# Two-part stores of the mirrored features in a fused attention, Fourier and MLP kernel

## Chip, cores and metric

One core of one Trainium2 chip runs the whole program in one launch. The metric is the device time of an execution in microseconds (us). Everything is float32 in DRAM; matmul operands are float32, or pairs of reduced-precision parts ("hi" and "lo", called h and l in the names).

## What is computed

```python
def _attn_ref(q, k, v, tau):                      # 4 batches, 8 heads, 576 rows, 64 columns
    scores = scale * np.matmul(q, k.transpose(0, 1, 3, 2))
    thresh = np.max(scores, axis=-1, keepdims=True) - tau
    scores = np.where(scores >= thresh, scores, -1000000000.0)
    ...
    return np.matmul(attn, v).astype(np.float32)

def _moe_ref(x, w_ch1, w_ch2):                    # x: 4 x 576 x 512
    X = np.fft.fft(x, axis=1)
    X = np.fft.fft(X, axis=2)
    u = x + np.real(X).astype(np.float32)
    ...
    un = (u - mu) / np.sqrt(var + 1e-06)
    ch = np.maximum(un @ w_ch1, 0.0) @ w_ch2      # 512 -> 2048 -> 512
    return (u + ch).astype(np.float32)

def _moe2_ref(x, w_val, conv_w, w_out):
    ...
    return (gate * val @ w_out).astype(np.float32)  # gate: sigmoid of a 5-tap convolution
```

## The kernel before

Features lie on partitions, sequence positions on the free axis. Attention runs first, in 16 head pairs (`p`, four to a batch `b`) of 9 score tiles each. A tile (`g_tile`) is scores on TensorE (`s`, L686), row maximum on VectorE (`neg`, L751), exponential on ScalarE (`e`, L757), threshold and sum on VectorE (`p`, L768), scaling on GpSimd (`p`, L776), transposes on TensorE (`t`, L788) and a copy to SBUF (`m`, L805). `g_pv` then multiplies with the values (L455), and ScalarE copies the result into `xt` (L460), 128 features by 576 positions.

When the four pairs of a batch are there, `g_fold` and `g_fft` make the real part of the two-dimensional Fourier transform. Symmetry halves it: features 0 to 255 and the features that mirror them, 256 to 511 in the kernel's own order, come out of the same two products (L598): their difference `dd` and sum `sm` (L628, L630). `g_odd` reads a block of 128 attention features back from DRAM (`xd`, L654) and its mirrored block (`xr`, L655), adds `dd` and `sm` on GpSimd (L634 and L636 into `xd`, L639 and L641 into `xr`) and stores both to `u_d[b]`, a DRAM buffer of 512 features by 576 positions (L637 and L643). There are two blocks to a batch, `j` = 0 and 1. Row 0 of the mirrored block 0 is feature 256, the middle one, which belongs to another path (`g_ny`, L616); so for `j` = 0 the store L643 leaves row 0 out and carries 127 rows, 2,304 bytes each.

In batches 0 to 2 the tiles of `j` = 1 use the same buffers as those of `j` = 0: the loads L654 and L655 of `j` = 1 must wait until the stores L637 and L643 of `j` = 0 have landed. In batch 3 `j` = 1 has buffers of its own.

The MLP's weights come from DRAM in 32 pieces by GpSimd's queue (`raw`, L945), are split into hi and lo on VectorE, ScalarE and GpSimd (L280 to L290), and those of the first 16 pieces are stored (`e_h`, `e_l`, L969) and loaded again into the weight tiles `w0h`, `w0l`, `w1h`, `w1l` (L929) as soon as attention's buffers come free. Chunk 0 of the MLP (512 positions) is woven into the end of attention and of batch 3's Fourier transform: `h` (L1258) needs `w0h` and `w0l`, `c` (L1294) needs `w1h` and `w1l`. Four more chunks (L1104, L1120), the gate and the output product (L1492, L1510) follow, TensorE running through.

The order of instructions on each engine is set when the program is built: a planner (`Loom`) with costs and due times writes it once, and no cost of it depends on the DMAs of L643. All DMAs but those of GpSimd are issued by SyncE (SP), which takes its list strictly in order: an entry that waits holds all that stand behind it. SP's DMAs rotate through eight completion semaphores, so that each also waits until the one eight before it has landed.

Of the kernel before, what the change touches and what calls it, by code (L numbers as in the profile page):

```python
# [23 lines left out]
DM = H * D  # L24
# [50 lines left out]
def dve(n, fast=False):  # L75
    return 137.0 + (0.54 if fast else 1.055) * n
# [242 lines left out]
def attention_fft(tc, right, ps_f, a, u_d, dram, conv_w, loom):  # L319
    nc = tc.nc  # L320
    PE, DVE, ACT, POOL, SP = nc.tensor, nc.vector, nc.scalar, nc.gpsimd, nc.sync
    right1 = ExitStack()
    with ExitStack() as right2, ExitStack() as right2b, ExitStack() as right3, ExitStack() as right4, ExitStack() as scores, ExitStack() as turned:
# [208 lines left out]
        def g_fft(b):  # L532
# [68 lines left out]
            def buffers(j):  # L601
                if b < B - 1 or j == 0:
                    return ([fft_p.tile([128, S], F32, tag=nm, name=nm) for nm in ("xd", "xr")]
                            + [fft_p.tile([128, KE], F32, tag=nm, name=nm) for nm in ("ws", "dd", "sm")])
                wide = [f32(fft_p.tile([128, 2, KE], F32R, tag=nm, name=nm)) for nm in ("xeh", "xel", "xoh", "xol")]
                return [t.rearrange("p a b -> p (a b)")[:, 0:S] for t in wide[:2]] + [wide[2][:, 0], wide[2][:, 1], wide[3][:, 0]]
# [18 lines left out]
            def g_odd(j, f, room, x, xr, ws, dd, sm):  # L625
                yield "after", ("ws", b, j)
                yield "DVE", dve(KE), 0.25
                DVE.tensor_tensor(out=dd, in0=ws, in1=f[:, 0:KE], op=ALU.subtract)  # L628
                yield "DVE", dve(KE), 0.25
                DVE.tensor_tensor(out=sm, in0=ws, in1=f[:, 0:KE], op=ALU.add)  # L630
                loom.free(room)
                up, dn, md = slice(0, HALF + 1), slice(S - 1, HALF, -1), slice(1, HALF)
                yield "POOL", 860.0, 3, "port"
                POOL.tensor_tensor(out=x[:, up], in0=x[:, up], in1=dd[:, up], op=ALU.add)  # L634
                yield "POOL", 780.0, 3, "port"
                POOL.tensor_tensor(out=x[:, dn], in0=x[:, dn], in1=sm[:, md], op=ALU.add)  # L636
                SP.dma_start(out=u_d[b][j * 128:(j + 1) * 128], in_=x)  # L637
                yield "POOL", 860.0, 3, "port"
                POOL.tensor_tensor(out=xr[:, up], in0=xr[:, up], in1=sm[:, up], op=ALU.add)  # L639
                yield "POOL", 780.0, 3, "port"  # L640
                POOL.tensor_tensor(out=xr[:, dn], in0=xr[:, dn], in1=dd[:, md], op=ALU.add)  # L641
                r = int(j == 0)
                SP.dma_start(out=u_d[b][DM // 2 + 128 * j + r:DM // 2 + 128 * j + 128], in_=xr[r:])  # L643
                loom.mark("added", b, j)

            yield ("after", *[("part", b, k, nb) for k in range(2) for nb in range(3)])
# [3 lines left out]
            for j in range(2):  # L650
                if j and b < B - 1:
                    yield "after", ("added", b, 0)
                x, xr, ws, dd, sm = buffers(j)
                SP.dma_start(out=x, in_=xs[j * 128:(j + 1) * 128])  # L654
                SP.dma_start(out=xr, in_=rev[j * 128:(j + 1) * 128])  # L655
                if b % 2 and j == 0:
                    ny = fft_p.tile([2, S], F32, tag="ny", name="ny")
                    for i, t in enumerate((ny_d, rev)):
                        SP.dma_start(out=ny[i:i + 1], in_=t[0:1])
                    f, room = yield from stage2(False, slice(0, CE, CE - 1))  # L660
                    loom.add(g_ny(f, room, ny))
                f, room = yield from stage2(False, slice(1 + j * 128, 129 + j * 128))
                loom.add(g_even(j, f, room, ws))
                f, room = yield from stage2(True, slice(j * 128, j * 128 + 128))
                loom.add(g_odd(j, f, room, x, xr, ws, dd, sm))
# [1017 lines left out]
```

## Time and profile before

| | us |
|---|---|
| median of 3 runs | 859.88 |
| lowest, highest run | 858.81, 861.76 |
| profiled execution, its time | 858.65 |
| its span, first to last instruction | 856.9 |
| TensorE busy (share of the span) | 817.6 (95%) |
| VectorE, ScalarE, GpSimd busy | 561.7, 418.0, 380.1 |
| mean granted clock of TensorE | 0.993 |

The profile is of one execution, with an entry for every instruction. A wait of an engine is the time that it stood still before an instruction, with the event that ended it; "<-" reads "by". In a timeline a row is a start, a length, the engine, the line, what is written from what, and how many were merged into the row. SP's rows show when it issued a DMA, not when the DMA landed; the landing shows where something waits for it.

### The profile page before, as it was taken

Reading aid. Unit: us, or ns where it says so; the run is one execution under the profiler, and the core shown is the slowest. Engines: PE = TensorE matmul, PEld = TensorE weight load, DVE = VectorE, ACT = ScalarE, POOL = GpSimd, SP = SyncE. Lnnn points to the kernel's source line nnn. Section 1 sums busy time; section 2 is a strip of 40 time slices with the busy share of each in tenths; the row PEclk is TensorE's granted clock in tenths of the full one; section 3 lists DMA queues with packets and bytes.
Section 4 is the critical chain, followed back from the end, with each engine's and each line's share of the span. In section 5 each row is a group of like instructions: output and inputs, shape, how many; then the busy total and the mean of one; then the engine's idle time right before and its main releaser. Section 6 shows DMA issues by size and latency. Waiting matters only on the chain.

```text
span 856.9 us, 13836 instructions
## 1 busy us (share of the span) xinstructions
PE 817.6 (95%) x4878; PEld 651.3 (76%) x4878; DVE 561.7 (66%) x1220; ACT 418.0 (49%) x845; POOL 380.1 (44%) x448
## 2 busy tenths in 40 slices
PE   8999999999889997999999999999999999999997
PEld 6555566556556754788899999998888788889986
DVE  7999899999898996688847732142123656328730
ACT  5778777777577774644545323133122331133432
POOL 4556864884688556475452431013003110075421
PEclk9999999999999998999999999999999999999999
DMA  6365365535534539968634622003000230532111
GB/s 214 106 211 186 104 184 176 185 131 194 188 111 154 211 95 362 370 228 294 219 129 168 218 60 66 1 24 113 1 1 10 95 105 0 195 128 83 62 50 62
DMA packets 63661, 117.67 MB, mean 137 GB/s; under 512 B 14304, under 2 KB 21472, under 8 KB 63592
## 3 DMA queue, kind: packets, MB, share of 16 engines
q1 hardware_dynamic: 56248, 92.93, 32.3%
q0 software_dynamic: 7200, 23.86, 8.2%
q8 instruction: 39, 0.64, 0.3%
q14 instruction: 30, 0.25, 0.1%
q10 hardware_dynamic: 144, 0.00, 0.0%
HBM read 85.29 MB, written 31.47 MB: 136 GB/s over the span
## 4 chain that ended last, share of the span: by engine, by line
PE 70%; DVE 15%; ACT 5%; issue 5%; POOL 3%; DMA 2%; SPq 0%; DVEq 0%; ACTq 0%; POOLq 0%
PE c L1120 16%; PE h L1104 16%; DVE neg L751 6%; PE s L686 5%; PE f L455 5%; PE o L1510 5%; PE h L1258 5%; PE v L1492 5%; PE c L1294 4%; DVE p L768 4%; PE t L788 3%; ACT e L757 2%; PE f L598 2%; PE f L583 1%; DMA w0h<-e_h 1%
## 5 line engine op out<-in xcount | busy, mean ns | idle before, releaser
L776 POOL TENSOR_SCALAR p<-p,su 128x576 f32<-128x576 f32 x144 | 110.0, 773 | 87.8 <-DVE su L703 79.1
L1108 DVE SCALAR_TENSOR_TENSOR hl<-h,hh 128x384 fp32r<-128x384 f32 (+1 forms) x64 | 39.8, 622 | 147.4 <-ACT hh L1107 147.4
L1107 ACT ACTIVATE hh<-h 128x384 fp32r<-128x384 f32 (+1 forms) x64 | 34.9, 545 | 203.2 <-PE h L1104 202.9
L757 ACT ACTIVATE e<-s,neg 128x576 f32<-128x576 f32 x144 | 102.2, 742 | 53.9 <-DVE neg L751 47.9
L768 DVE SCALAR_TENSOR_TENSOR p<-s,thr,e 128x576 f32<-128x576 f32 x144 | 112.2, 815 | 8.4 <-POOL p L776 0.2
L751 DVE TENSOR_REDUCE neg<-s 128x1 f32<-128x576 f32 x144 | 102.7, 748 | 8.7 <-PE s L686 8.0
L686 PE MATMUL s<-kt,qt 64*128 64x288 f32 (+1 forms) x640 | 97.8, 440 | 9.3 <-DVE p L768 8.7
L1120 PE MATMUL c<-hl,w1h 128*128 128x384 f32 (+1 forms) x256 | 92.9, 363 | 0.2 <-DVE hl L1108 0.2
L1120 PE MATMUL c<-hh,w1h 128*128 128x384 f32 (+1 forms) x256 | 92.6, 362 | 0.0
L1120 PE MATMUL c<-hh,w1l 128*128 128x384 f32 (+1 forms) x256 | 92.6, 362 | 0.0
L788 PE MATMUL t<-ident,p 128*128 128x128 f32 x464 | 69.3, 282 | 13.8 <-ACT m L805 9.8
L686 PEld LDWEIGHTS s<-kt,qt 64*128 64x128 f32 (+1 forms) x640 | 45.9, 175 | 47.0 <-issue 17.7
L788 PEld LDWEIGHTS t<-ident,p 128*128 128x128 f32 x464 | 50.9, 142 | 36.3 <-issue 17.4
L455 PE MATMUL f<-m,v 128*64 128x320 f32 (+1 forms) x512 | 68.8, 410 | 0.2 <-ACT th L723 0.2
L805 ACT ACTIVATE m<-t 128x512 f32<-128x512 f32 x116 | 66.0, 599 | 1.1 <-PE t L788 0.6
L1104 PE MATMUL h<-unh,w0h 128*128 128x384 f32 (+1 forms) x256 | 61.6, 362 | 0.0
L1104 PE MATMUL h<-unh,w0l 128*128 128x384 f32 (+1 forms) x256 | 61.6, 362 | 0.0
L1104 PE MATMUL h<-unl,w0h 128*128 128x384 f32 (+1 forms) x256 | 61.5, 362 | 0.0
L1129 POOL TENSOR_TENSOR res<-ht,res 128x512 f32<-128x512 f32 (+1 forms) x20 | 23.0, 1187 | 84.5 <-DVE ht L1128 84.5
L455 PEld LDWEIGHTS f<-m,v 128*64 128x64 f32 x512 | 34.0, 137 | 25.8 <-issue 3.6
L1120 PEld LDWEIGHTS c<-hl,w1h 128*128 128x128 f32 x256 | 48.1, 188 | 6.1 <-DVE hl L1108 1.2
L1120 PEld LDWEIGHTS c<-hh,w1l 128*128 128x128 f32 x256 | 48.0, 188 | 5.0
(268 smaller groups left out, 1701.2 us busy)
## 6 DMA issues: line engine op xcount, KB each, us to landing
raw<-in_moe_w_ch POOLq DMA_DIRECT2D x32, 512.0 KB, 6.6
qt<-in_q SPq DMA_DIRECT2D x15, 576.0 KB
kt<-in_k SPq DMA_DIRECT2D x15, 432.0 KB
ypad<-y_d SPq DMA_DIRECT2D x16, 288.0 KB
out<-os SPq DMA_DIRECT2D x18, 256.0 KB
v<-in_v SPq DMA_DIRECT2D x16, 256.0 KB
e_h<-cx SPq DMA_DIRECT2D x16, 256.0 KB
e_l<-ct SPq DMA_DIRECT2D x16, 256.0 KB
```

Source lines behind the costliest of these rows:

```text
L455: PE.matmul(out=f[h * 64:h * 64 + 64, 0:n], lhsT=w, rhs=r, start=(t == 0), stop=(t == 4))
L686: PE.matmul(out=s[o, c, 0:HALF], lhsT=qt[w, hh, q], rhs=kt[w, 2 if h == 2 and hh else hh], start=True, stop=True)
L751: DVE.tensor_reduce(out=neg[u][:, j, 0:1], in_=sc[g][:, :, 0:HALF], axis=AX.XY, op=ALU.max, negate=True)
L757: ACT.activation(e, sc[g][:, :, 0:HALF], AF.Exp, bias=neg[u][:, j, 0:1], scale=1.0)
L768: DVE.scalar_tensor_tensor(out=p_view(g).rearrange("p (a b) -> p a b", a=2), in0=sc.pop(g)[:, :, 0:HALF], scalar=thr[u][:, j:j + 1], in1=e ...
L776: POOL.tensor_scalar(out=v, in0=v, scalar1=ssum[u][:, j:j + 1], scalar2=1.0, op0=ALU.mult, op1=ALU.mult)
L788: PE.matmul(out=f[:, t, :], lhsT=pv[:, t * 128:(t + 1) * 128], rhs=ident, is_transpose=True, start=(t == 0), stop=(t == 3))
L805: ACT.activation(o, fv, AF.Copy)
L1104: PE.matmul(out=f[:, 0:n], lhsT=ww[:, k * 128:(k + 1) * 128], rhs=x[:, k, 0:n], start=(i == 0), stop=(i == 3 * KB - 1))
L1120: PE.matmul(out=ch[c][o][:, 0:n], lhsT=ww[:, o * 128:(o + 1) * 128], rhs=x, start=(at_ == 0 and i == 0), stop=(at_ == FB - 1 and i == 2))
L1258: PE.matmul(out=f[:, 0:n], lhsT=ww[:, k * 128:(k + 1) * 128], rhs=x[:, k, 0:n], start=(i == 0), stop=(i == 3 * KB - 1))
L1492: PE.matmul(out=f[:, 0:HALF], lhsT=w[:, k, o * 128:(o + 1) * 128], rhs=x[:, k, s], start=(i == 0), stop=(i == 3 * KB - 1))
```

## The change

The one store of rows 1 to 127 becomes two, rows 1 to 15 and rows 16 to 127. The same bytes go to the same place; for `j` = 1 the slice is the whole tile, as before.

```diff
-                r = int(j == 0)
-                SP.dma_start(out=u_d[b][DM // 2 + 128 * j + r:DM // 2 + 128 * j + 128], in_=xr[r:])
+                for r in ([slice(1, 16), slice(16, 128)] if j == 0 else [slice(0, 128)]):
+                    SP.dma_start(out=u_d[b][DM // 2 + 128 * j:][r], in_=xr[r])
                 loom.mark("added", b, j)
```

In the built program the instructions of TensorE, VectorE, ScalarE and GpSimd stand in the same order as before. SP's list gets one entry more in each of the four batches.

SP's list in batch 2, before, from the store of `j` = 0 on. (`DMAHW` are the eight completion semaphores; `PE`, `Pool`, `DVE`, `Activation` are counters of the engines. The number at a name tells buffers apart.)

```order
L643 DMA u_d_59<-xr 127x576 [waits DMAHW3_49,Pool_49]
L654 DMA xd<-xs_2634 128x576 [waits DMAHW6_49,DMAHW4_49]
L655 DMA xr<-xr_2635 128x576 [waits DMAHW7_49,DMAHW5_49]
L390 DMA v_195<-in_v 128x512 [waits DMAHW0_49,PE_49]
L392 DMA vt_196<-in_vt 64x64 [waits DMAHW1_49,PE_49]
L392 DMA vt_196<-in_vt 64x64 [waits PE_49]
L487 DMA xr_3651<-xt 128x576 [waits Activation_49]
```

L655 holds SP here until the store above it has landed (DMAHW5), and everything below it with it.

The same place in the changed program:

```order
L643 DMA u_d_59<-xr 15x576 [waits DMAHW5_49,Pool_49]
L643 DMA u_d_59<-xr 112x576 [waits DMAHW0_49]
L654 DMA xd<-xs_2635 128x576 [waits DMAHW6_49,DMAHW1_49]
L655 DMA xr<-xr_2636 128x576 [waits DMAHW7_49,DMAHW2_49,DMAHW0_49]
L390 DMA v_195<-in_v 128x512 [waits DMAHW3_49,PE_49]
```

L655 now waits for the landing of both parts (DMAHW2 and DMAHW0); nothing else has moved.

What follows on SP, from the changed program (in the program before, the same entries in the same order; only the semaphores are counted on by one):

```order
L969 DMA e_h<-cx 128x512 [waits DVE_49]
L969 DMA e_l<-ct 128x512 [waits Pool_49]
L474 DMA mirror<-xr_3653 128x576 [waits DMAHW6_49,DMAHW1_49]
L474 DMA mirror<-xr_3653 128x576 [waits DMAHW2_49]
L929 DMA w0h_4216<-e_h 128x512 [waits DMAHW3_49]
L929 DMA w1l_4219<-e_l 128x512 [waits PE_49]
L637 DMA u_d_59<-xd 128x576 [waits DMAHW7_49,Pool_49]
L643 DMA u_d_59<-xr 128x576 [waits DMAHW0_49,Pool_49]
L969 DMA e_h<-cx 128x512 [waits DMAHW1_49,DVE_49]
L969 DMA e_l<-ct 128x512 [waits DMAHW2_49,Pool_49]
L495 DMA xs_3652<-xt 128x576 [waits DMAHW3_49,Activation_49]
L929 DMA w0h_4337<-e_h 128x512 [waits DMAHW4_49]
```

The engine counters in it name these instructions: the first `e_l` waits for GpSimd's L290 of the same piece, `w1l` for the last scores of attention (L686), the stores L637 and L643 of `j` = 1 for L636 and L641, the second `e_l` for the next L290, `xs` for ScalarE's copy L460 of pair 14. The last row, `w0h` of the second weight group, is the load that the second `h` (L1258) needs.

## Rows read from the trace of the kernel before

**Rows 1.** The page's busy times by engine.

```profile
PE 817.6 (95%) x4878; PEld 651.3 (76%) x4878; DVE 561.7 (66%) x1220; ACT 418.0 (49%) x845; POOL 380.1 (44%) x448
```

**Rows 2.** TensorE's waits from 326 to 860 us: total, times, longest.

```profile
PE h L1258 <- DMA w0h<-e_h: 5.0, 1, 5.0
PE f L583 <- ACT sp L560: 1.0, 1, 1.0
```

**Rows 3.** The chain that ended last, 300 to 345 us: start, us, what.

```profile
329.75 9.32 DMA w0h<-e_h
...
339.12 4.92 PE h L1258 x12
```

**Rows 4.** Busy time by engine in stretches, then granted clock, DMA share, GB/s.

```profile
139.40:153.30 13.90, 13.09 (x100) 8.94 (x101) 12.56 (x33) 11.27 (x25) 7.42 (x10) 1.00 0.19 65
...
329.70:334.00 4.30, 4.30 (x24) 2.71 (x20) 4.30 (x6) 3.67 (x8) 3.21 (x5) 1.00 1.04 406
334.00:339.10 5.10, 0.13 (x1) 0.00 (x0) 3.47 (x4) 1.21 (x3) 4.40 (x7) 0.74 1.04 399
```

**Rows 5.** The same for L1258 alone (TensorE, weight loads, clock, DMA).

```profile
339.10:343.90 4.80, 4.79 (x12) 3.60 (x12) 0.57 1.05 395
...
376.10:378.90 2.80, 2.77 (x12) 2.10 (x12) 1.00 0.96 358
```

**Rows 6.** SP's waits over the whole span: total, times, longest.

```profile
SPq L655 <- DMA u_d<-xr: 26.6, 3, 9.1
...
SPq L474 <- DMA xr<-xt: 6.0, 2, 5.3
```

**Rows 7.** SP's timeline in batch 2 (start, length of the issue, line, DMA).

```profile
301.91 0.32 SPq L637 DMA_DIRECT2D u_d<-xd  x1
303.31 0.24 SPq L643 DMA_DIRECT2D u_d<-xr  x1
303.99 4.35 SPq L654 DMA_DIRECT2D xd<-xs  x1
317.14 0.32 SPq L655 DMA_DIRECT2D xr<-xr  x1
...
329.14 0.46 SPq L495 DMA_DIRECT2D xs<-xt  x1
329.75 0.58 SPq L929 DMA_DIRECT2D w0h<-e_h  x1
```

**Rows 8.** GpSimd's waits, 139 to 170 us.

```profile
POOL kt L381 <- DMA kt<-in_k: 1.2, 1, 1.2
```

**Rows 9.** GpSimd's timeline, 300 to 400 us.

```profile
313.36 1.04 POOL L290 TENSOR_TENSOR ct<-raw 128x512 fp32r<-128x512 f32 x1
...
318.00 0.80 POOL L634 TENSOR_TENSOR xd<-xd,dd 128x289 f32<-128x289 f32 x1 [0.49 <-DMA xd<-xs]
...
321.02 0.96 POOL L639 TENSOR_TENSOR xr<-xr,sm 128x289 f32<-128x289 f32 x1 [1.58 <-DMA xr<-xr]
...
324.67 1.20 POOL L290 TENSOR_TENSOR ct<-raw 128x512 fp32r<-128x512 f32 x1
```

**Rows 10.** TensorE's timeline, 300 to 341 us.

```profile
315.74 1.40 PE L686 MATMUL s<-kt,qt 64*128 64x288 f32 x12
...
323.87 0.66 PE L788 MATMUL t<-ident,p 128*128 128x128 f32 x4 [0.43 <-POOL p L776]
324.75 0.66 PE L788 MATMUL t<-ident,p 128*128 128x128 f32 x4 [0.23 <-POOL p L776]
...
333.06 1.07 PE L1258 MATMUL h<-unl,w0h 128*128 128x512 f32 x4
```

**Rows 11.** ScalarE's timeline, 316 to 380 us.

```profile
323.48 0.44 ACT L460 ACTIVATE xt<-f 128x320 f32<-128x320 f32 x1 [1.59 <-PE f L455]
...
344.07 0.60 ACT L1270 ACTIVATE hh<-h 128x512 fp32r<-128x512 f32 x1 [8.62 <-PE h L1258]
```

**Rows 12.** VectorE's timeline, 316 to 380 us.

```profile
344.70 0.69 DVE L1272 SCALAR_TENSOR_TENSOR hl<-h,hh 128x512 fp32r<-128x512 f32 x1 [6.76 <-ACT hh L1270]
```

## Prediction

> **What bounds the kernel now.** I read the page's busy times first: TensorE is busy 817.6 us of the 856.9 of the span [rows 1], so a change that touches no engine's work can pay only where TensorE stands still, or where its clock is low. TensorE's waits from the end of attention on are next [rows 2]: one of 5.0 us, before the second `h` (L1258), ended by the DMA that brings `w0h`; the next longest is 1.0 us, in the 520 us behind it. The chain that ended last runs through the same place: the load of `w0h` stands in it with 9.32 us, and the `h` behind it with 4.92 us for 12 matmuls [rows 3]. The stretch table tells the rest of that pause. While TensorE rests, DMA is full (share 1.04, 399 GB/s) [rows 4]; after it the 12 matmuls take 4.79 us at a granted clock of 0.57, close to the 1.2 GHz level, where the same 12 take 2.77 us at 1.00, the 2.4 GHz level, later [rows 5]. So the pause costs 5.0 us and then 4.79 - 2.77 = 2.0 us of low clock: 7.0 us.
>
> Why does `w0h` come late? It was issued at 329.75 [rows 7], and SP issues in order. SP's own waits show that L655 waited three times for `u_d<-xr`, the 127-row store, 26.6 us together [rows 6]. In batch 2 the store was issued at 303.31 and L655 at 317.14, 13.8 us later; L654, between them, needed 4.35 us to issue [rows 7]. The 128-row store of the same bytes per row just before it, `u_d<-xd` at 301.91, had landed when L654, which waits for it, was issued at 303.99: at most 2.1 us [rows 7]. One row less takes over six times as long.
>
> **The change part by part.**
>
> *The store itself, batches 0 to 2.* Two DMAs instead of one. What a 15-row and a 112-row store take no row shows. From below: the 128-row store, 2.1 us [rows 7]. From above: 13.8 us, that of the 127 rows [rows 7]. I take 2 to 6 us: 128-row stores with other traffic beside them reach the 5.3 us that `mirror` waited for one [rows 6], and 112 rows are nearer to 128 than to 127 only if the number of DMA engines that share the rows decides; that is the one assumption of this forecast, and the rival below prices its failure. The Trainium skill gives a rule for just this (DMA: Bandwidth & Descriptors, the section "Why a DMA increments its semaphore by 16 and not by 1"): a DMA from SP is spread over the largest number of engines, up to 16, that divides its rows, so 127 rows go through one engine, 15 rows through 15 and 112 through 16. By that rule the value is the lower end; the 13.8 against 2.1 us agree with it, though no row here shows 15 or 112 rows.
>
> The extra issue costs SP 0.24 to 0.32 us [rows 7], hidden in the wait that it shortens. L655 in batch 2 then issues between 303.6 + 2.1 = 306 and 310, not at 317.14.
>
> *What holds SP next.* Behind L655, four things stand that do not depend on the store. The first `e_l` waits for GpSimd's L290, which ends at 313.36 + 1.04 = 314.4 [rows 9]; so whether L655 goes at 306 or 310 makes no difference. `w1l` waits for attention's last scores, 315.74 + 1.40 = 317.1 [rows 10]. The stores of `j` = 1 wait for L636 and L641: L634 began at 318.00 after 0.49 us for `xd`, L639 at 321.02 after 1.58 us for `xr` [rows 9], both loads that now land early, so that the L641 store comes at about 320.5. The second `e_l` waits for the next L290, which ended at 324.67 + 1.20 = 325.9 [rows 9] and comes some 2 us sooner with those waits gone; and `xs` waits for ScalarE's copy, 323.48 + 0.44 = 323.9 [rows 11], where it was issued at 329.14 [rows 7]. So `w0h` is issued at about 324.6 and not at 329.75: 5.1 us sooner. The 11 us at L655 are worth 5 at `w0h`.
>
> *When `w0h` lands.* It took 9.32 us with DMA full [rows 3, 4]. Had it the same now, it would land at 333.9; with an idle queue, by the 2.1 us above, at 326.7. What queued ahead of it (`mirror` twice, the first weight group, the stores, some 3 MB by their shapes) leaves from 314.4 on and no longer in a bunch after 317, so I take about 329. TensorE wants it at the end of the first `h`, 333.06 + 1.07 = 334.1 [rows 10], less what it gains before (next).
>
> *GpSimd's earlier scaling.* With 0.49 and 1.58 us less waiting [rows 9] GpSimd reaches L776 about 2 us sooner, and TensorE's two waits for it, 0.43 and 0.23 us [rows 10], go: -0.7 us. The first `h` then ends at 333.4.
>
> *Batches 0 and 1, and batch 3.* The same stall is covered there: TensorE is busy 13.09 us of the 13.90 between store and release in batch 0, VectorE 12.56 [rows 4], and of GpSimd's waits behind it only one names a load, `kt`, 1.2 us [rows 8]. I take 0, with 0 to 2 us for both. In batch 3 no load waits for the store, and TensorE does not wait behind it [rows 2]: 0. If that cover were gone, SP would still be sooner than before.
>
> *What is late next.* With the pause gone TensorE reaches everything behind it 7.7 us sooner. The engines that feed it there were waiting for it: ScalarE 8.62 us for `h` [rows 11], VectorE 6.76 us for ScalarE [rows 12]. They move with it. The next weights have to come sooner too: the DMAs whose issue the L655 wait pushed behind 317 are, by their shapes, seven blocks of 0.26 to 0.29 MB and the first weight group, 1.05 MB: some 3 MB, or 7.5 us at the 399 GB/s of the full queue [rows 4]. So DMA can follow by about as much as TensorE gains, with nothing much to spare. I charge 0, and up to 2 us for the range.
>
> **The sum**, against the profiled execution: 5.0 + 2.0 + 0.7 = 7.7 us less, 858.65 - 7.7 = 851.0. That execution lies 1.2 us under the median of the runs, 859.88; on the median's scale the forecast is 859.88 - 7.7 = **852.2 us**.
>
> **Rivals.**
>
> *A part of the pause stays.* `w0h` lands 9.32 us after its issue again, at 333.9 [rows 3], 0.5 us after TensorE wants it, or later weights come late, up to 2 us. For it speaks the full DMA [rows 4], against it the 5 us of unhurried queue before. If the clock falls in the short pause as it did in the long one, 7.7 - 0.5 - 2.0 = 5.2 us remain: about 854.7.
>
> *DMA takes it back.* From 329.7 the queue is full at about 400 GB/s [rows 4]. If the release moves up not 3 MB but 1 MB, because GpSimd and TensorE hold SP at the places named, TensorE gains 2.5 us at the next weights whatever happens at `w0h`: about 857.4. Against it: of the holds only two, 314.4 and 317.1, lie before the first weights, and both are sooner than the issues that they replace.
>
> *The change does not do what it says, and costs.* If the landing goes by rows and not by how they divide, 13.8 us for 127 is 0.11 us a row: 1.6 us for 15 rows and 12.2 for 112, one behind the other, and each with an end of its own, up to the 2.1 us of a whole short store [rows 7]. L655 then goes at 317.4 to 319.5, `w0h` follows by 0.3 to 2.3 us, and TensorE's pause grows from 5.0 to as much as 7.3: 860.2 to 862.2, slower; it decides as soon as L655 goes later than 317.14. Batches 0 and 1 are covered as now. Against it stands the 128-row store in 2.1 us. By the rule of the page named above it cannot be.
>
> *More than forecast.* The first two stalls give the 1.2 us of `kt` [rows 8] and as much again in batch 1: 849.8.
>
> **How the numbers follow.** About 0.3% (2.6 us) is what a measurement of this kernel can tell from no change. Chances: the forecast 0.67, part of the pause 0.13, more than forecast 0.08, DMA takes it back 0.07, slower store 0.05. The first three are faster by over 0.3%: 0.88. DMA's rival lies on the edge, 0.05 of it within and 0.02 over; the slow store is 0.03 within and 0.02 slower. So 0.90, 0.08, 0.02. The range for 8 in 10 goes from the last rival, 849.8, to the half pause with the scatter of the runs, 1.2 us, on it: 854.7 + 1.2 = 855.9.
>
> **What would show it.** Right: SP's wait of L655 for `u_d<-xr` falls from 26.6 us to under 10; L655 in batch 2 issues before 311; `w0h` of the second group issues near 324.6; TensorE's 5.0 us wait at L1258 is gone, and the 12 matmuls there take 2.8 us at a clock of 1.00. If L655 still waits some 9 us each time, the store is not faster and the first step fell. If `w0h` is early and TensorE pauses at a later `h` or `c`, DMA took it back. If all that holds and the time falls by less than 5 us, something behind 365 us lost it, which no row here shows.

## The result, and the profile after

The changed kernel takes 850.75 us (median of 4 runs, 850.53 to 851.17) against 859.43 us (4 runs of the kernel before beside it, 858.81 to 861.76): a ratio of 0.9895, 95% interval 0.9875 to 0.9914, or 7.4 to 10.7 us less. Between the medians it is 8.7 us; 7.7 us less were forecast. The profiled execution took 851.17 us, with a span of 849.4.

The page's busy times by engine: hardly an engine works less than before [rows 1]; the span is shorter.

```profile
PE 816.8 (96%) x4878; PEld 651.4 (77%) x4878; DVE 561.2 (66%) x1220; ACT 418.0 (49%) x845; POOL 381.2 (45%) x448
```

TensorE's waits from 318 to 855 us (what waits, for what: total, times, longest). The 5.0 us for `w0h` of [rows 2] are not there; the 1.0 us at L583 is now the longest:

```profile
PE f L583 <- ACT sp L560: 1.0, 1, 1.0
```

SP's waits over the span. L655's for the store fell from 26.6 us [rows 6] to 7.3. The wait for GpSimd's `ct`, 47.7 us before, took most of that over: SP is released earlier and then stands at the next thing that is not ready.

```profile
SPq L969 <- POOL ct L290: 62.5, 19, 10.4
...
SPq L655 <- DMA u_d<-xr: 7.3, 4, 2.7
```

SP's timeline in batch 2 (start, length of the issue, line, DMA), to be read against [rows 7]. All of it lies 1.2 us later in this execution than in the profile of before: the first store here begins at 303.12, there at 301.91.

```profile
303.12 0.32 SPq L637 DMA_DIRECT2D u_d<-xd  x1
304.53 0.76 SPq L643 DMA_DIRECT2D u_d<-xr  x2
305.38 0.39 SPq L654 DMA_DIRECT2D xd<-xs  x1
308.75 0.34 SPq L655 DMA_DIRECT2D xr<-xr  x1
...
315.63 0.32 SPq L969 DMA_DIRECT2D e_l<-ct  x1
...
318.42 0.44 SPq L929 DMA_DIRECT2D w1l<-e_l  x1
...
321.57 0.32 SPq L643 DMA_DIRECT2D u_d<-xr  x1
...
325.98 0.32 SPq L969 DMA_DIRECT2D e_l<-ct  x1
...
326.82 0.44 SPq L929 DMA_DIRECT2D w0h<-e_h  x1
...
333.45 0.32 SPq L969 DMA_DIRECT2D e_h<-cx  x1
```

L655 goes 4.2 us behind the store instead of 13.8, and L654 issues in 0.39 us instead of 4.35. The `w0h` of the second group follows at 326.82; on the clock of the profile of before, that is 325.6 instead of 329.75.

TensorE's timeline at the place of the pause (start, length, line, operation, count): the second `h` begins at 334.22, straight behind the first, and its 12 matmuls end at 336.94, 2.7 us later, where they took 4.79 us [rows 5].

```profile
333.30 1.08 PE L1258 MATMUL h<-unl,w0h 128*128 128x512 f32 x4
334.22 1.07 PE L1258 MATMUL h<-unh,w0h 128*128 128x512 f32 x4
...
336.94 0.39 PE L1294 MATMUL c<-hh,w1h 128*128 128x512 f32 x1
...
339.66 1.07 PE L1258 MATMUL h<-unh,w0h 128*128 128x512 f32 x4
```

The stretch table (length, busy times of PE, PEld, DVE, ACT, POOL, then granted clock, DMA share, GB/s), against [rows 4]: the DMAs run at 305 GB/s from 317.1 to 329.7 (275 in the profile of before), and when the queue is full from 334 on, TensorE is busy all the time at a clock of 1.00.

```profile
317.10:329.70 12.60, 12.39 (x108) 7.42 (x110) 12.01 (x23) 7.16 (x18) 9.63 (x12) 1.00 0.94 305
...
334.00:339.10 5.10, 5.10 (x24) 4.24 (x23) 4.45 (x7) 2.06 (x4) 4.40 (x6) 1.00 1.05 366
```

### The profile page after: what moved, and what is told of

Its sections match the earlier page's. It is cut to its first block, busy times and chain, and to the rows that moved or that the text cites. A ratio compares the mean times of both kernels' runs of the same rounds, so it can differ in the third digit from the quotient of the medians.

```text
span 849.4 us, 13837 instructions
## 1 busy us (share of the span) xinstructions
PE 816.8 (96%) x4878; PEld 651.4 (77%) x4878; DVE 561.2 (66%) x1220; ACT 418.0 (49%) x845; POOL 381.2 (45%) x448
## 4 chain that ended last, share of the span: by engine, by line
PE 70%; DVE 16%; ACT 4%; DMA 3%; POOL 3%; issue 3%; SPq 0%; DVEq 0%; ACTq 0%; POOLq 0%
PE c L1120 18%; PE h L1104 18%; DVE neg L751 6%; PE o L1510 5%; PE s L686 5%; DVE p L768 5%; PE v L1492 4%; PE c L1294 4%; PE f L455 4%; PE h L1258 4%; PE t L788 3%; ACT e L757 2%; PE f L598 1%; PE f L583 1%; DMA w0l<-e_l 1%
## 5 line engine op out<-in xcount | busy, mean ns | idle before, releaser
L686 PE MATMUL s<-kt,qt 64*128 64x288 f32 (+1 forms) x640 | 98.4, 441 | 8.9 <-DVE p L768 8.2
L686 PEld LDWEIGHTS s<-kt,qt 64*128 64x128 f32 (+1 forms) x640 | 46.1, 176 | 47.0 <-issue 17.1
```

The source lines that it names most:

```text
L686: PE.matmul(out=s[o, c, 0:HALF], lhsT=qt[w, hh, q], rhs=kt[w, 2 if h == 2 and hh else hh], start=True, stop=True)
```

## The experiments

Each edit is to the kernel before. The kernel before took 860.28 us (19 runs, 858.65 to 862.29) beside the runs of the first two groups, and 860.29 us (19 runs, 858.77 to 861.88) beside the 128-row store, the buffer of its own and the 20 extra matmuls.

### Two parts in batch 2 alone, and in the others alone

```diff
-                r = int(j == 0)
...
+                for r in ([slice(0, 128)] if j else [slice(1, 16), slice(16, 128)] if b == 2 else [slice(1, 128)]):
+                    SP.dma_start(out=u_d[b][DM // 2 + 128 * j:][r], in_=xr[r])
```

> Only batch 2 stores in two parts; batches 0, 1 and 3 keep the 127-row store. Theory (the gain comes through the weight load that batch 2's stall delays): all of it, about 851 us, TensorE's 5.0 us wait at L1258 gone, SP's two waits of L655 in batches 0 and 1 still about 9 us each. Rival (every one of the four stores gives its share): a quarter to a half of the gain, 855 to 857 us.

The other has `b != 2` there:

> Batches 0, 1 and 3 store in two parts; batch 2 keeps the 127-row store. Theory: no gain, 858.5 to 859.5 us, the 5.0 us wait at L1258 still there; the stalls of batches 0 and 1 vanish and nothing on TensorE moves by more than some tenths of a us. Rival (each store its share): 852 to 855 us.

Batch 2 alone: 852.2 us (4 runs), ratio 0.9915, 0.9891 to 0.9939. The others alone: 859.52 us (10 runs), ratio 0.9992, 0.9982 to 1.0002. So batch 2 carries the gain, and the others give between nothing and 1.5 us; 0.6 us of that lie, in the profile, at the very end of the program (see the account of the prediction). SP's timeline of the others alone in batch 2, and TensorE's wait:

```profile
304.80 0.24 SPq L643 DMA_DIRECT2D u_d<-xr  x1
...
318.68 0.32 SPq L655 DMA_DIRECT2D xr<-xr  x1
```

```profile
PE h L1258 <- DMA w0h<-e_h: 5.4, 1, 5.4
```

There SP's waits at L655 fell by half as well (26.6 to 13.9 us), and TensorE's pause stayed: what is saved at a wait counts only where somebody stands behind it.

### Two parts that divide badly: 14 + 113 rows, 5 + 122 rows

```diff
+                for r in ([slice(1, 15), slice(15, 128)] if j == 0 else [slice(0, 128)]):
+                    SP.dma_start(out=u_d[b][DM // 2 + 128 * j:][r], in_=xr[r])
```

> The stores in two parts as in the change, but cut one row further up: rows 1 to 14 and 15 to 127, 14 and 113 rows. Theory (the number of engines that a store runs on is the largest number up to 16 that divides its rows): 113 rows run on one engine, 113 x 0.109 = 12.3 us, so that L655 in batch 2 still goes some 12 us after the store and w0h comes 1 to 2 us sooner than before: 857 to 858.5 us, with a pause of 3 to 4 us at L1258. Rival (two smaller stores side by side, or not starting a long store at row 1, is what helps): as the change, about 851 us.

With `slice(1, 6), slice(6, 128)`:

> Rows 1 to 5 and 6 to 127, 5 and 122 rows. Theory: 122 = 2 x 61, two engines, 61 x 0.109 = 6.6 us, so that L655 in batch 2 goes some 7 us after the store, at about 311, still ahead of the hold of SP by GpSimd's L290 at 314.4: the full gain, about 851 us. Rival (the time goes with the length of the stall): half the gain, about 855 us.

14 + 113: 858.38 us (10 runs), ratio 0.9977, 0.9962 to 0.9992. 5 + 122: 852.44 us (4 runs), ratio 0.9905, 0.9890 to 0.9920. SP's timeline of 14 + 113, then of 5 + 122:

```profile
303.79 0.62 SPq L643 DMA_DIRECT2D u_d<-xr  x2
...
316.62 0.34 SPq L655 DMA_DIRECT2D xr<-xr  x1
```

```profile
303.91 0.58 SPq L643 DMA_DIRECT2D u_d<-xr  x2
304.63 0.34 SPq L654 DMA_DIRECT2D xd<-xs  x1
312.03 0.34 SPq L655 DMA_DIRECT2D xr<-xr  x1
...
315.17 0.48 SPq L969 DMA_DIRECT2D e_l<-ct  x1
...
326.22 0.44 SPq L929 DMA_DIRECT2D w0h<-e_h  x1
```

One row moved from the first part to the second brings the stall back: 12.8 us from store to L655, and a wait of 4.6 us at the second `h`, more than the 3 to 4 us expected. So it is not the cutting that helps. With 5 + 122 the stall is only cut to 8.1 us, yet the whole gain is there: L655 at 312.03 is just early enough, since SP reaches the `e_l` behind it at 315.17, 0.2 us after the L290 that it has to wait for in any case (313.96 + 1.03). `w0h` issues 22.3 us behind the store, as with 15 + 112 (326.82 - 304.53).

Times alone leave a rival open: the larger part starts at row 1, 15, 6, 16 or 0 where it has 127, 113, 122, 112 or 128 rows, and as the two add up to 128, the start divides by 2, 4, 8 or 16 just where the count does. The trace settles it. SP's queue (packets, MB, share of 16 engines) from 311 to 312.5 us of before, with the 127 rows under way, from 308.5 to 311.5 with 5 + 122, and from 304.55 to 304.9 with 14 + 113, when the 14 rows go:

```profile
q1 hardware_dynamic: 17, 0.04, 6.6%
```

```profile
q1 hardware_dynamic: 66, 0.15, 12.8%
```

```profile
q1 hardware_dynamic: 23, 0.03, 36.3%
```

One engine of 16 is 6.25%: the 127 rows go through one engine, the 122 through two, and the 14 keep some 5.8 busy at once (0.363 x 16) though they start at row 1. The number of rows decides, not where they start.

### One store of 128 rows

```diff
+                for r in ([slice(1, 16), slice(16, 128)] if j == 0 and b % 2 else [slice(0, 128)]):
+                    SP.dma_start(out=u_d[b][DM // 2 + 128 * j:][r], in_=xr[r])
```

> In batches 0 and 2 one store of all 128 rows (row 0 is written again later by L616), in batches 1 and 3 the two parts. Theory (all that counts is that the store lands in 2 to 6 us): as the change, 850.5 to 851.2 us, L655 in batch 2 some 2 us after the store. Rival (the second, smaller part costs something by itself): up to 0.5 us less than the change.

851.74 us (4 runs), ratio 0.9902, 0.9882 to 0.9921: as the change. SP's timeline in batch 2, where the store has 128 rows:

```profile
304.34 0.32 SPq L643 DMA_DIRECT2D u_d<-xr  x1
...
308.69 0.32 SPq L655 DMA_DIRECT2D xr<-xr  x1
```

L655 goes 4.3 us behind the store, not the 2 us expected, and as late as with two parts (4.2). So the second DMA costs nothing that can be measured.

### A buffer of its own for the second mirrored block

```diff
-                    return ([fft_p.tile([128, S], F32, tag=nm, name=nm) for nm in ("xd", "xr")]
+                    return ([fft_p.tile([128, S], F32, tag=nm, name=nm) for nm in (("xd", "xr2") if b == 2 and j else ("xd", "xr"))]
```

> The kernel before with its 127-row stores, but in batch 2 the mirrored block of j = 1 has a buffer of its own, so that L655 waits for no store. Theory (the slow store also holds one DMA engine, through which a share of every later DMA of SP has to go, and the first e_l, eight DMAs behind the store, waits for it too): SP stops again until the store has landed at about 317, at e_l; w0h then comes 2 to 3 us sooner than before and TensorE's pause shrinks to 2 to 3 us: 854 to 857 us. Rival (only L655's wait matters): the full gain, about 851 us.

858.4 us (10 runs), ratio 0.9980, 0.9970 to 0.9990: 1.9 us, less than either theory had. SP's timeline in batch 2, and its waits:

```profile
305.39 0.24 SPq L643 DMA_DIRECT2D u_d<-xr  x1
306.07 4.35 SPq L654 DMA_DIRECT2D xd<-xs  x1
310.47 0.65 SPq L655 DMA_DIRECT2D xr<-xr  x1
...
319.26 0.32 SPq L969 DMA_DIRECT2D e_l<-ct  x1
```

```profile
SPq L969 <- DMA u_d<-xr: 4.9, 1, 4.9
```

L655 no longer waits for the store, and goes at 310.47. But the store is as slow as before, and stops SP at two other places: L654's issue still takes 4.35 us, and the `e_l` at 319.26, the eighth DMA behind the store and so on the same completion semaphore, now waits for it, 13.9 us behind it. `mirror` waits another 3.5 us, for the `xr<-xt` that was issued behind the slow store, and goes at 323.42; 4.4 us of the pause stay. The wait at L655 was the place where the slow store showed; taking the dependence away there moves it.

### Work in the pause: 20, 23 and 12 extra matmuls, and the kernel before once more

```diff
+                    if j == 1:
+                        for _ in range(20):
+                            PE.matmul(out=f[:, 0:n], lhsT=w[0][0][0][:, 0:128], rhs=uh[:, 0, 0:n], start=True, stop=True)
```

> The kernel before, with 20 more matmuls of 512 columns on TensorE between the first and the second h of chunk 0 (their result is overwritten), so that TensorE works through most of its 5.0 us pause there. Theory (2.0 us of the gain are the low clock behind the pause): the weights come no sooner, the pause is filled, the 12 matmuls of the second h take 2.8 us and not 4.8: about 857.4 us, 2.0 less than before. Rival (the 12 matmuls are slow for the full DMA beside them, or the clock falls anyway): no change, 859.4 us.

> The kernel before with 23 instead of 20 extra matmuls (L1258 and L1259, into the tile that the second h then starts anew, so the output stays the same) in TensorE's pause: 23 x 0.235 = 5.4 us of work. It settles what the run with 20 left open. Theory 1, the later landing there was scatter: w0h lands 8.0 to 8.4 us after the first h begins, as in the two profiles of the unfilled kernels, the extra work then ends just before or after it, TensorE's wait at the second h is under 0.6 us, its 12 matmuls take 2.8 to 3.1 us, and the time falls by 1.3 to 2.0 us to about 858.5. Theory 2, a busy TensorE beside the full DMA delays the landing: w0h lands 8.7 us or more after the first h begins, a wait of 0.3 to 1 us stays, and the time falls by under 1 us. In both the granted clock stays at 1.00.

> The kernel before with 12 extra matmuls (L1258 and L1259, into the tile that the second h then starts anew, so the output stays the same) in TensorE's pause: 12 x 0.235 = 2.8 us of work. With 20 and with 23 the second h began 1.31 and 1.33 us after the last extra matmul, and w0h seemed to land later the more of them there were (9.94 and 10.67 us after its issue, against 9.27 to 9.44 in three profiles without them). Theory 1: it is a fixed time behind the extra work, not the load, that ended the pause there; with 12 the load decides again, 9.3 to 9.5 us after its issue, and 2.0 to 2.6 us of the wait stay. Theory 2: each extra matmul delays the load by some 0.03 to 0.05 us; then w0h lands 9.7 to 10.0 us after its issue and 2.5 to 3.0 us stay. In both: if 2 us of rest already lower the clock, the 12 matmuls take 4.4 us or more and the time is within 0.7 us of before; if not, they take 2.8 to 3.1 us and the time falls by 1 to 2 us, which would show the 2.0 us of low clock to be worth that in the total.

> The kernel before, unchanged, profiled a second time, to see how far two profiles of one program differ. If the 5.0 us of the pause are the same in every execution, the wait for w0h is 4.9 to 5.1 us, and 43.2 to 43.4 us pass from the 127-row store to the third h, as in the first profile. If the landing of w0h under the full DMA scatters, the wait lies anywhere from 4.6 to 5.8 us, and that stretch with it, as it did in the run with the store unsplit in batch 2 (5.4 and 44.1 us). The time is 858.7 to 862.3 us in both.

| extra matmuls | us, median (runs) | ratio, 95% interval | wait at the second `h` | its 12 matmuls | `w0h`, issue to landing |
|---|---|---|---|---|---|
| 20 | 859.95 (10) | 0.9996, 0.9986 to 1.0006 | 1.33 us | 3.04 us | 9.94 us |
| 23 | 860.32 (11) | 0.9997, 0.9987 to 1.0007 | 1.31 us | 3.02 us | 10.67 us |
| 12 | 861.54 (12) | 1.0018, 1.0004 to 1.0033 | 3.39 us | 4.61 us | 10.29 us |
| none, again | 860.64 (1) | | 4.86 us | 4.99 us | 9.44 us |

The kernels before beside the runs with 23 and 12 took 860.24 us (15 runs) and 860.79 us (17 runs). The stretch table of the 12 matmuls of the second `h`, with 20, then with 12 (columns as above):

```profile
340.80:343.90 3.10, 3.08 (x13) 2.55 (x14) 0.00 (x0) 0.01 (x1) 0.00 (x0) 1.00 1.05 398
```

```profile
343.40:348.10 4.70, 4.64 (x13) 3.70 (x14) 0.00 (x0) 0.00 (x0) 0.00 (x0) 0.64 1.04 397
```

The cause of the low clock is settled. With the same full DMA beside them (398 and 397 GB/s) the 12 matmuls ran at a granted clock of 1.00, the 2.4 GHz level, after TensorE had rested for 1.3 us, and at 0.64, for the most part the 1.2 GHz level, after a rest of 3.4 us. The low clock comes from the rest, not from the traffic. What it costs shows in its stretch. TensorE's second and third `h` with 20 (L1258 is L1261 in this kernel):

```profile
340.82 1.20 PE L1261 MATMUL h<-unh,w0h 128*128 128x512 f32 x4 [1.33 <-DMA w0h<-e_h]
...
346.41 1.07 PE L1261 MATMUL h<-unh,w0h 128*128 128x512 f32 x4
```

From the one to the other 5.59 us pass with 20 and 5.57 with 23, against 7.20 with 12 and 7.55 with none: 2.0 us. In the total they do not show; all three runs missed the gain that I expected. In these profiles the second `h` began 1.0, 1.8 and 1.2 us later behind the store (20, 23, 12) than with none, because `w0h` was issued 0.4 to 0.5 us later and then landed 0.5 to 1.2 us later than the 9.44 us above. The later issue is about what profiles without extra matmuls show (26.3 to 26.8 us behind the 127-row store of batch 2, here 26.7 to 26.9). There the landing took 9.27 to 9.73 us, 9.73 with 14 + 113, so that with one profile each a part of the later landing can be scatter. With 20 and 23 this takes back part of the 2 us; with 12 the low clock is there as well. Twelve delay the load more than twenty, so it is not a fixed price for each, and neither theory on the landing holds as it stood: with 12 it was later than theory 1 allows, and the order is not theory 2's. The queue of instructions between the issue and the landing of `w0h`, for 23:

```profile
q8 instruction: 1, 0.02, 0.7%
```

Each of the kernels with extra matmuls has one packet of instructions on q8 in that stretch, and in the profiles in which the pause stayed without them there is none. 0.7% of 16 engines over 10.67 us is 1.2 us of one engine; `w0h` is late by 1.2 us with 23, but by 0.5 and 0.9 with 20 and 12. That the packet delays it was not tried by itself: why the landing moved stays open.

## Why the prediction was right, point by point

Two profiles of one program do not start alike (the last section), so the stretches are measured from the first issue of the store at L643 on. The kernel before, profiled again, gives this in SP's and in TensorE's timeline (first, second and third `h`):

```profile
305.26 0.24 SPq L643 DMA_DIRECT2D u_d<-xr  x1
```

```profile
333.16 1.21 PE L1258 MATMUL h<-unh,w0h 128*128 128x512 f32 x4
...
341.07 2.08 PE L1258 MATMUL h<-unh,w0h 128*128 128x512 f32 x4 [4.86 <-DMA w0h<-e_h]
...
348.62 1.07 PE L1258 MATMUL h<-unh,w0h 128*128 128x512 f32 x4
```

In the changed kernel the first `h` began at 331.35.

| stretch | before, again | after | gain | forecast |
|---|---|---|---|---|
| store to first `h` | 27.90 | 26.82 | 1.1 | 0.7 |
| first to second `h` (the pause) | 7.91 | 2.87 | 5.0 | 5.0 |
| second to third `h` (low clock) | 7.55 | 5.44 | 2.1 | 2.0 |
| third `h` to the end of the span | 510.3 | 509.7 | 0.5 | 0 |

*The store.* 2 to 6 us were taken, 4.2 were measured. The lower end, 2.1 us, was reached by no form: 128 rows take 4.3 us at this place too. In the changed kernel a packet of instructions (q8) takes 1.6 us of one engine between the store and L655 (2.3% of 16 engines over 4.3 us), and none falls on the store that landed in 2.1 us; that this makes the difference was not tried. The assumption on which it rested, that the number of engines that share the rows decides, is shown by the times of five forms and by the queue's shares. By the Trainium skill (DMA: Bandwidth & Descriptors, "Why a DMA increments its semaphore by 16 and not by 1") the largest share of rows on one engine is 127 for 127 rows, 113 for 14 + 113, 61 for 5 + 122, and 8 for 128. The measured times from store to L655, 13.8, 12.8, 8.1 and 4.3 us, follow that order, by an estimate from these shares some 0.08 us a row ((13.8 - 4.3) / 119). The rule agrees with the trace, one engine for 127 rows and two for 122. The rival "the landing goes by rows", which wanted the two parts as slow as one, fell.

*What holds SP next.* All holds but one stood where they were put, 1.2 us later by the clock of this execution: `e_l` at 315.63, straight behind L290 (314.57 + 1.04), `w1l` at 318.42, the store of `j` = 1 at 321.57. That L655's time within these bounds does not matter is shown by 5 + 122. The one that was mis-sized is the second `e_l`: I had its L290 come some 2 us sooner and ScalarE's copy hold `xs` last. GpSimd did lose both its waits, but that L290 came only 1.1 us sooner:

```profile
318.69 0.79 POOL L634 TENSOR_TENSOR xd<-xd,dd 128x289 f32<-128x289 f32 x1
320.10 0.79 POOL L639 TENSOR_TENSOR xr<-xr,sm 128x289 f32<-128x289 f32 x1
324.75 1.20 POOL L290 TENSOR_TENSOR ct<-raw 128x512 fp32r<-128x512 f32 x1
```

It ends at 325.95, and `e_l` goes at 325.98, `w0h` behind it. So `w0h` was 4.1 us sooner (325.6 on the clock of before), not 5.1.

*When `w0h` lands.* At about 333.4, 6.6 us behind its issue: the `e_h` that SP issues at 333.45 is the eighth DMA behind it and waits for its landing, as the same `e_h` did before (339.13, with the landing that ended TensorE's wait).

```profile
SPq L969 <- DMA w0h<-e_h: 1.8, 1, 1.8
```

TensorE wanted it at 334.22, so 0.8 us were to spare. The forecast had 4.4 us for the landing and 4.4 us to spare (329 against 333.4): this term was mis-sized, and that it cost nothing was in part luck. A landing as slow as the 9.32 us of [rows 3] would have come at 336.1 and left 1.9 us of the pause: the rival "a part of the pause stays" was nearer than the chance given to it says. What speaks for the reason given, bytes that leave earlier, is the stretch of 13.8 us from the store on, before and after:

```profile
303.30:317.10 13.80, 13.34 (x97) 8.51 (x95) 12.99 (x32) 9.48 (x21) 7.14 (x10) 1.00 0.22 65
```

```profile
304.50:318.30 13.80, 13.35 (x97) 8.50 (x95) 12.98 (x32) 9.48 (x21) 7.13 (x11) 1.00 0.56 175
```

At 175 GB/s and not 65 some 1.5 MB more had moved by then (13.8 x 110). No run changed the queue alone.

*DMA takes it back* did not happen: no wait for a weight stands in TensorE's waits after.

*GpSimd's earlier scaling* was worth 1.1 us, not 0.7: both waits of [rows 10] are gone. In the profile of before that the table uses they are 0.8 us and not 0.66; where the other 0.3 us came from nothing in the rows tells.

*Batches 0, 1 and 3, and the end*: 0 was taken, and the run without batch 2 shows 0.7 us with an interval that takes in 0. "More than forecast" by the first two stalls is not shown. The half microsecond behind the third `h` is a term that the forecast lacks. It lies behind ScalarE's last copy to `os` (L1513), where SP waits for the last stores of `out`, before, then after:

```profile
SPq L1679 <- DMA out<-os: 1.5, 1, 1.5
```

```profile
SPq L1679 <- DMA out<-os: 0.9, 1, 0.9
```

From the start of that copy to the end of the span 4.3 us pass in both profiles of before and with the buffer of its own, 4.3 with one more DMA on SP (batch 2 alone), 4.1 with two more (128 rows), 3.7 with three (the others alone) and 3.6 with four (the change, 14 + 113, 5 + 122). So it goes with the number of SP's DMAs and not with how their rows divide; by what way no run shows. Most of what the others alone gave is this.

*The low clock.* The 2.0 us are in the stretch from the second to the third `h`, 2.1. Its cause is shown by the extra matmuls, and so is its price in that stretch (5.59 and 5.57 us against 7.55); as a gain of the total it was measured only together with the pause.

## What to carry to other kernels

A store from SP whose number of rows no number from 2 to 16 divides took three times as long here as one with more rows (13.8 against 4.3 us). Cut it so that the larger part divides by 16, or write the row that is not needed. Then look where it holds an in-order queue, and follow the queue to the next hold: here 9.6 us saved between store and L655 were 4.1 at the load that mattered, cutting the stall to 8.1 us gave all of it, and the same saving in batches 0 and 1 gave nothing that shows. Removing the waiter's dependence instead of the slow transfer gave 1.9 us, since the wait moved to the next place that needs the same transfer.

## What was not expected of the hardware

*The start differs from run to run of one program.* The first eight score matmuls, before any instruction that was changed, in the kernel before (profiled again) and in the one with batch 2 alone:

```profile
5.60 2.13 PE L686 MATMUL s<-kt,qt 64*128 64x288 f32 x8
```

```profile
5.60 1.41 PE L686 MATMUL s<-kt,qt 64*128 64x288 f32 x8
```

The same work took 1.24 us in the first profile of before and 2.29 in that of the changed kernel, which moves all of the trace by a microsecond. It is not the only such place: with 12 extra matmuls these eight took 1.49 us, and the store, still ahead of any changed instruction, came at 306.43, 3.1 us later than in the first profile of before. Two traces should be laid over each other at an instruction close to the change, not at 0.

*A slow store reaches past its reader.* While the 127 rows are under way, the issue of the next DMA on SP takes 4.35 us (L654) where it takes 0.34 to 0.39 us with 15 + 112 or 5 + 122; why is not shown. And a store of other data, `e_l` in the kernel with a buffer of its own, waits 4.9 us for it: in this program the eighth DMA behind another shares its semaphore.

*Extra work in a pause that a load ends gave nothing*: in one profile each the load landed 0.5 to 1.2 us later, and with 12 extra matmuls the kernel was 0.18% slower than before. Of the 2.4 us by which that profile is longer than that of before, taken again, 1.2 lie ahead of the store, where nothing was changed, so the matmuls need not be the whole cause.
